# The last 64 output features of a projection as pairs of heads in two 64-column tiles

## The chip, the core and the metric

The kernel runs on one core of a Trainium2 chip. A core has five engines with queues of their own: TensorE (PE in the profile, with its weight loads listed apart as PEld), VectorE (DVE), ScalarE (ACT), GpSimd (POOL) and SyncE (SP), which issues most transfers. Each engine works through its own list of instructions in order and waits on semaphores that the others raise. The metric is the time of one execution on the device in microseconds; lower is better.

## The reference, cut to what matters

A token matrix x of 2048 x 576 goes through four residual layers, A, B, A, B. Layer A is attention over eight dilated neighbours. Layer B, which the change is about, is recurrent: it works on segments of 32 tokens, and eight memory rows come out of one segment and go into the next.

```python
for s in range(n_seg):                                   # 64 segments
    h = jnp.concatenate([mem, xs], axis=1)               # 8 memory rows, 32 tokens
    q, k, v = (jnp.einsum('btd,dhe->bhte', h, W) for W in (Wq, Wk, Wv))   # 32 heads of 128
    p = _softmax(masked(q @ k * scale))
    o = jnp.einsum('bhqk,bhke->bhqe', p, v)
    o = jnp.einsum('bhte,hed->btd', o, Wo)               # the output projection: 32 heads, 576 features
    mem = o[:, :M, :]                                    # the next segment needs these rows
    outs.append(o[:, M:, :])
```

## The kernel before

The two B layers run as two lanes side by side, the second five segments behind the first (`DLY`). There are 64 + 5 = 69 steps (`b_step`). In 59 of them both lanes are at work and a step has 80 columns: 40 of lane 0 and 40 of lane 1 (8 memory rows and 32 tokens each). In the first five and the last five steps only one lane is at work; the operations there are on 40 or 48 columns. The blocks of layer A (`a_tile`) fill in between.

A step consists of these parts, each a function: `qk` (Q and K of all heads, the lines 842 and 845), `vpass` (V, line 889, in four tiles of 32 columns of the array), `scores` (lines 921, 925 and 931, again in tiles of 32 columns), `softmax` on DVE, ACT and POOL, `pv` (line 972, in tiles of 32 rows), and `oproj`, the output projection. `pv` runs twice, for the halves r = 0 and r = 1 of the heads; ACT and DVE copy its results into the tile `OT`.

`oproj` computes psY = sum over 32 heads of Wo[h]^T OT[h]. The 576 output features go onto partitions, so they are five blocks of 128 rows side by side in one PSUM tile `psY`, 80 columns each. 576 is four and a half blocks: the fifth matmul of a head takes 64 features of its own and, as rows 64 to 127, 64 weights of the next head, whose result nobody reads. So a head costs five matmuls of 128x128 weights by 80 columns, and a step 160. They are issued in eight groups (`k` = 0 to 7) of four heads, 20 matmuls each. Group k waits for the copy `o_ev[k]` into `OT`; groups 0 to 3 use the half r = 0 and groups 4 to 7 the half r = 1.

Two functions take the result out of `psY`, both on DVE. `mem_out` (lines 1015 to 1017) copies the memory columns into `hT` of the next step, which its `qk` waits for. `x_out` (line 1035) adds the token columns to the residual stream.

The order of all instructions is fixed when the program is built. `_Plan` is a list scheduler: every operation has an engine, a duration in us that is written in the source, a priority, dependences (`deps`) and buffers. At each moment the free engine takes the ready operation with the lowest priority value; matmuls of another array tiling (`mode`) than the running one pay `SWITCH`. The constants in `PR` shift the priorities of each kind of operation. The plan sets the order only. The waits in the program are put in afterwards by the framework: where an instruction writes or reads a tile that one on another engine has used, it waits for that one, whether the plan named that dependence or not.

Of the kernel before, what the change touches and what calls it, by code (L numbers as in the profile page):

```python
# [8 lines left out]
F32 = mybir.dt.float32  # L9
BF16 = mybir.dt.bfloat16  # L10
ACT = mybir.ActivationFunctionType
ALU = mybir.AluOpType
# [4 lines left out]
P = 128  # L17
SEG = 32
NM = 8
W80 = 80  # L20
# [3 lines left out]
MC = 32  # L24
NH = 32
D = 576
# [25 lines left out]
class _Plan:  # L52
# [41 lines left out]
    def run(self, log=None):  # L94
# [51 lines left out]
        while left:  # L146
            moved = True
            while moved:
                moved = False
                for e, heap in ready.items():  # L150
# [81 lines left out]
def _act(n):  # L232
    return 0.22 + 0.00072 * n
# [13 lines left out]
class _K:  # L247
# [37 lines left out]
    def setup(self):  # L285
        nc, tc = self.nc, self.tc
        cp = self.pool("const", 1)
# [58 lines left out]
        def tiles(name, n, shape, dt=BF16):  # L346
            ts = [wp.tile(shape, dt, name=f"{name}{i}") for i in range(n)]
            self.pl.pool(name, ts)
            return ts
# [13 lines left out]
        tiles("x1", 2, [P, 5, T], F32)  # L363
        tiles("x3", 2, [P, 5, T], F32)
        tiles("x5", 1, [P, 5, T], F32)
        tiles("x0", 1, [P, 640])
        tiles("xs", 1, [P, 5, 2, T])
        tiles("st", 1, [P, 2, T], F32)
# [155 lines left out]
    def a_tile(self, layer, j, dep, due, span):  # L524
# [5 lines left out]
        def pr(f):  # L530
            return due - span * (1.0 - f)
        Q = PR["A"]
        if layer == 1:
# [451 lines left out]
    def oproj(self, t, prios):  # L985

        nc, pl = self.nc, self.pl
        psY = self.psY = pl.buf("r")
        c0, c1 = self.cols(t)
        o = None  # L990
        for k in range(8):
            def mm(e, k=k):
                for h in range(4 * k, 4 * k + 4):
                    for mb in range(5):
                        w0 = h * D + mb * P
                        nc.tensor.matmul(psY.t[:, mb * W80 + c0:mb * W80 + c1], lhsT=self.wo[:, w0:w0 + P], rhs=self.OT[:, h % 16 // 4 * 8 + h // 16 * 4 + h % 4, c0:c1],  # L996
                                         start=(h == 0 and mb == 0), stop=(h == NH - 1 and mb == 4), skip_group_check=True)
            ot = self.ot[k // 4]
            o = pl.op("PE", 0.717 if c1 - c0 == W80 else 0.58, mm, prios[k], [o, self.wo_in[k // 2], self.o_ev[k]],
                      acq=[psY] if k == 0 else (), uses=[ot] if k == 0 else [psY, ot], lat=0.0 if k < 7 else None, mm=20)  # L1000
        return o

    def mem_out(self, t, dep, prio):

        nc, pl, psY = self.nc, self.pl, self.psY
        act = [l for l in range(2) if self.lane_seg(t, l) is not None and self.lane_seg(t + 1, l) is not None]
        if not act or t + 1 >= self.nsteps:
            return
        hT = self.hT[t + 1]
        a, b = act[0] * NM, (act[-1] + 1) * NM  # L1010

        def cp(e):
            y = psY.t[:, 0:5 * W80].rearrange("p (c n) -> p c n", c=5)
            w = slice(MC + a, MC + b)
            nc.vector.tensor_copy(out=hT.t[:, 0:4, w], in_=y[:, 0:4, w])
            nc.vector.tensor_copy(out=hT.t[0:64, 4, w], in_=y[0:64, 4, w])
            nc.vector.tensor_copy(out=hT.t[64:128, 5, w], in_=y[0:64, 4, w])
        o = pl.op("DVE", 0.56, cp, prio, [dep, self.gate[t + 1]], uses=[psY, hT])
        self.mem_in.setdefault(t + 1, []).append(o)

    def x_out(self, t, dep, prio):

        nc, pl, psY = self.nc, self.pl, self.psY
        for lane in range(2):
            s = self.lane_seg(t, lane)
            if s is None:
                continue
            xT, ld, xb = self.acc[lane][s // NS]
            w = slice((s % NS) * SEG, (s % NS + 1) * SEG)

            def add(e, lane=lane, xT=xT, xb=xb, w=w):
                x = xT.t[:, :, w]
                o = x if xb is None else xb.t[:, 0:5 * T].rearrange("p (c n) -> p c n", c=5)[:, :, w]
                c0 = XC[lane]
                nc.vector.tensor_tensor(out=o, in0=x, in1=psY.t[:, 0:5 * W80].rearrange("p (c n) -> p c n", c=5)[:, :, c0:c0 + SEG], op=ALU.add)
            self.x_done[lane][s] = pl.op("DVE", 0.34, add, prio, [dep, ld], uses=[psY, xT] + ([] if xb is None else [xb]))

    def b_step(self, t):
        self.qkt, self.qk_ev, self.PT, self.ot, self.o_ev = {}, {}, {}, {}, []
# [2 lines left out]
        for g in range(11):  # L1042
            self.qk(t, g, t + PR["qk"] + PR["qkd"] * g)
        self.vpass(t, 1, t + PR["v1"])
        self.vpass(t, 0, t + PR["v0"])
# [17 lines left out]
    def trace(self):  # L1063
# [28 lines left out]
        if VERBOSE:  # L1092
# [1 line left out]


DLY = 5
PR = dict(qk=0.371, qkd=0.051, v1=1.416, v0=0.716, w=-0.059, s0=0.01, s1=-1.032, p0=1.091, p1=-1.234, o=0.394,
          od=0.009, mo=0.162, xo=0.923, v2=2.122, a1=2.228, a1s=1.336, a2=0.41, a2s=7.809, fin=5.446, res=-4.695,
          ring=-6.459, A=(0.038, 0.482, 0.789, 0.731, 0.817, -0.034, 0.927, 0.994))
LEAD = 5  # L1100
COPY = 2
HOLD = False
# [58 lines left out]
```

## Time and profile before

| | |
|---|---|
| median of 9 runs | 2158.92 us |
| lowest and highest | 2154.22 and 2161.6 us |
| the profiled execution, its own time | 2162.85 us |
| its span, first to last instruction | 2161.2 us |
| granted TensorE clock, mean over the span | 0.983 |
| `oproj` matmuls (line 996) | 11040, of which 9440 with 80 columns and 1600 with 48 |

The span is the time from the first to the last instruction; 1.65 us of the execution lie around it. The profiled execution is 3.93 us above the median of the runs. A line of a timeline names the start in us, the length, the engine, the line of the source, the operation with its tiles, the shape and how many instructions were merged. Matmuls are pipelined: the length of one is its latency, about 0.2 us, while the next starts much sooner. What a group costs is therefore read from one group's start to the next one's start.

### The profile page before, as it was taken

How to read it: one execution, taken by the hardware profiler on the slowest of the kernel's cores; microseconds unless marked ns; L12 is line 12 of the kernel's file. 1: busy time of each engine (PE TensorE's matmuls, PEld its weight loads, DVE VectorE, ACT ScalarE, POOL GpSimd, SP SyncE). 2: the span in 40 equal slices, each digit the busy share in tenths (PEclk: the TensorE clock that was granted, in tenths of full speed). 3: DMA queues.
4: the chain of work that ended last, by engine and by line, in shares of the span. 5: the costliest groups of instructions: out<-in, count | busy, mean ns of one | idle time of the engine just before them, and what ended most of it. 6: DMA issues, size and time to landing. Idle time of an engine off the chain costs nothing.

```text
span 2161.2 us, 132215 instructions
## 1 busy us (share of the span) xinstructions
PE 2065.2 (96%) x60441; PEld 1733.3 (80%) x60441; DVE 1409.6 (65%) x3545; ACT 1171.8 (54%) x2855; POOL 925.1 (43%) x1310
## 2 busy tenths in 40 slices
PE   3688999999999999999999999999999999999997
PEld 3466888888888888888888888888888888888876
DVE  4556766666667666666766666666666666765674
ACT  2334555555556555555555555555555555554543
POOL 3135454454444444444444454444444444442220
PEclk7889999999999999999999999999999999999999
DMA  9654434343343333333433443344343334332110
GB/s 303 171 172 143 127 114 132 111 130 118 123 125 125 121 122 119 123 125 125 125 109 120 127 133 114 118 125 125 122 122 121 121 120 130 120 124 74 61 58 9
DMA packets 158303, 265.09 MB, mean 123 GB/s; under 512 B 23464, under 2 KB 89904, under 8 KB 157616
## 3 DMA queue, kind: packets, MB, share of 16 engines
q1 hardware_dynamic: 152000, 237.37, 35.4%
q0 software_dynamic: 4576, 18.88, 2.6%
q8 instruction: 472, 7.73, 1.5%
q14 instruction: 87, 0.71, 0.1%
q10 hardware_dynamic: 1168, 0.40, 0.1%
HBM read 240.46 MB, written 16.12 MB: 119 GB/s over the span
## 4 chain that ended last, share of the span: by engine, by line
PE 92%; DMA 4%; DVE 2%; issue 1%; ACT 1%; POOL 0%; SPq 0%; POOLq 0%; ACTq 0%; DVEq 0%
PE r L842 28%; PE r L996 18%; PE r L889 17%; PE r L582 7%; PE r L845 7%; PE r L972 3%; PE r L692 2%; PE r L921 2%; PE r L478 2%; DMA ring<-strip 2%; PE r L925 2%; PE r L656 1%; PE r L931 1%; DMA ring<-in_A_wqkv_dram 1%; PE r L631 1%
## 5 line engine op out<-in xcount | busy, mean ns | idle before, releaser
L842 PE MATMUL r<-hT,wk 128*128 128x80 bf16 (+1 forms) x8832 | 663.4, 199 | 7.8 <-DMA wk<-in_B_Wk_dram 5.9
L842 PE MATMUL r<-hT,wq 128*128 128x80 bf16 (+1 forms) x8832 | 661.3, 198 | 6.6 <-ACT hT L275 3.3
L842 PEld LDWEIGHTS <-wq 128*128 128x128 bf16 x8832 | 502.2, 99 | 39.6 <-issue 26.0
L845 PE MATMUL r<-hT,wqk_r 128*128 128x160 bf16 (+1 forms) x2208 | 507.7, 230 | 0.0
L275 ACT ACTIVATE qk<-r 128x480 bf16<-128x480 f32 (+2 forms) x626 | 332.8, 532 | 320.8 <-PE r L845 311.4
L842 PEld LDWEIGHTS <-wk 128*128 128x128 bf16 x8832 | 447.9, 100 | 7.1 <-DMA wk<-in_B_Wk_dram 6.0
L996 PE MATMUL r<-OT,wo 128*128 128x80 bf16 (+1 forms) x11040 | 422.5, 200 | 10.9 <-issue 6.8
L996 PEld LDWEIGHTS <-wo 128*128 128x128 bf16 x11040 | 396.6, 100 | 29.7 <-issue 16.6
L889 PE MATMUL r<-wv,hT 128*32 128x512 bf16 x5376 | 356.2, 384 | 2.8 <-POOL hT L277 1.7
L282 POOL TENSOR_TENSOR big<-qT,kT 128x512 bf16<-128x512 bf16 (+1 forms) x187 | 312.1, 1689 | 53.9 <-ACT kT L275 43.2
L282 POOL TENSOR_TENSOR ex<-ex,sum 128x384 bf16<-128x384 bf16 x137 | 115.2, 841 | 490.1 <-DVE sum L791 372.1
L282 POOL TENSOR_TENSOR big<-big 128x1280 bf16<-128x1280 bf16 (+1 forms) x66 | 129.9, 1969 | 398.9 <-DVE big L282 344.2
L889 PEld LDWEIGHTS <-hT 128*32 128x32 bf16 x6720 | 167.3, 96 | 136.1 <-issue 4.6
L780 DVE TENSOR_REDUCE nmx<-r 128x4 f32<-128x320 f32 (+1 forms) x276 | 143.1, 518 | 199.6 <-PE r L925 198.1
L275 ACT ACTIVATE V<-r 128x512 bf16<-128x512 f32 x305 | 182.0, 597 | 152.8 <-PE r L889 149.2
L845 PEld LDWEIGHTS <-wqk_r 128*128 128x128 bf16 x2208 | 220.0, 100 | 1.1 <-issue 1.1
L582 PE MATMUL r<-xn,ring 128*128 128x64 bf16 x4725 | 185.5, 194 | 16.7 <-DMA ring<-in_A_wqkv_dram 13.0
L275 ACT ACTIVATE OT<-r 128x320 bf16<-128x320 f32 (+1 forms) x372 | 137.4, 427 | 106.5 <-PE r L972 106.3
L582 PEld LDWEIGHTS <-ring 128*128 128x128 bf16 x4725 | 161.0, 98 | 36.2 <-issue 16.0
L781 DVE TENSOR_TENSOR r<-r,nmx 128x320 f32<-128x320 f32 (+1 forms) x276 | 147.0, 533 | 9.4
L275 ACT ACTIVATE big<-r 128x384 bf16<-128x384 f32 (+1 forms) x322 | 122.7, 450 | 45.4 <-issue 29.9
L277 DVE CAST OT<-r 128x320 bf16<-128x320 f32 (+1 forms) x180 | 76.2, 457 | 92.8 <-PE r L972 92.8
(150 smaller groups left out, 2967.2 us busy)
## 6 DMA issues: line engine op xcount, KB each, us to landing
ring<-strip SPq DMA_DIRECT2D x488, 320.0 KB, 3.4
ring<-strip SPq DMA_DIRECT2D x244, 160.0 KB, 3.8
x1T<-x SPq DMA_DIRECT2D x32, 160.0 KB, 4.1
x<-x1T SPq DMA_DIRECT2D x32, 160.0 KB, 3.4
x3T<-x SPq DMA_DIRECT2D x32, 160.0 KB, 4.0
x<-x3T SPq DMA_DIRECT2D x32, 160.0 KB, 3.6
wo<-in_B_Wo_dram POOLq DMA_DIRECT2D x4, 1152.0 KB, 34.6
wq<-in_B_Wq_dram POOLq DMA_DIRECT2D x2, 2048.0 KB, 17.7
```

The source lines that it names most:

```text
L275: nc.scalar.activation(out=out, in_=in_, func=ACT.Copy, scale=1.0 if scale is None else scale)
L277: (nc.vector if e == "DVE" else nc.gpsimd).tensor_copy(out=out, in_=in_)
L282: (self.nc.vector if e == "DVE" else self.nc.gpsimd).tensor_tensor(out=out, in0=in0, in1=in1, op=op)
L478: nc.tensor.matmul(psf, lhsT=(self.ones if c < 4 else self.ones_h)[:, :], rhs=xs.t[:, c].rearrange("p a t -> p (a t)"), start=(c == 0), st ...
L582: nc.tensor.matmul(ps.t[:, c * T:(c + 1) * T], lhsT=view()[:, kc, w0:w0 + P], rhs=xn.t[:, kc, :], start=(kc == 0), stop=(kc == 4))
L780: nc.vector.tensor_reduce(out=m, in_=v, axis=AX.X, op=ALU.max, negate=True)
L781: nc.vector.tensor_tensor(out=v, in0=v, in1=m.unsqueeze(len(shp) - 1).to_broadcast(shp), op=ALU.add)
L842: nc.tensor.matmul(pv[:, hh, wi, a:b], lhsT=self.Wb[wi][0][:, kc, h * P:(h + 1) * P], rhs=hT.t[:, kc, a:b], start=(hh == 0 and wi == 0 and ...
L845: nc.tensor.matmul(pv[:, hh, :, a:b], lhsT=self.Wb[0][1][:, h * P:(h + 1) * P], rhs=hT.t[:, 4:6, a:b], start=False, stop=(hh == n - 1), sk ...
L889: nc.tensor.matmul(ps.t[c * 32:(c + 1) * 32, :], lhsT=l, rhs=w, start=(kc == 0), stop=(kc == 4))
L972: nc.tensor.matmul(ps[c].t[:, i * n + a - c0:i * n + z - c0], lhsT=V[b].t[q4, r, i, :], rhs=pt.t[q4, i, b, a:z], start=(i == 0 and b == bl ...
L996: nc.tensor.matmul(psY.t[:, mb * W80 + c0:mb * W80 + c1], lhsT=self.wo[:, w0:w0 + P], rhs=self.OT[:, h % 16 // 4 * 8 + h // 16 * 4 + h % 4 ...
```

## The change

The 64 last features get matmuls of their own. A head now has four matmuls of 128x128 weights (features 0 to 511) in its group, 16 a group instead of 20. For features 512 to 575 a new operation `tails` issues, ahead of group 7, 32 matmuls with 128x64 weights, one a head. Even heads put their sum into partitions 0 to 63 of the fifth block of `psY`, odd heads theirs into partitions 64 to 127; these are two tiles of 64 columns of the array, and a new `mode` "D" in the plan. The wanted sum is that of the two.

The odd sum is copied by ACT into a new tile `half` (64 x 80 in SBUF). `mem_out` then copies the four full blocks, adds the two sums twice into `hT` (into chunk 4 and chunk 5), and a last DVE operation adds them in place in `psY`, for `x_out` to read. Three DVE operations a step become four, and there is one more ACT operation. All constants in `PR` have other values.

```diff
+        tiles("half", 1, [P, W80], F32)
...
+        def head(h, out, w0, n, start, stop):
+            nc.tensor.matmul(out, lhsT=self.wo[:, h * D + w0:h * D + w0 + n], rhs=self.OT[:, h % 16 // 4 * 8 + h // 16 * 4 + h % 4, c0:c1],
+                             start=start, stop=stop, skip_group_check=True)
+        tl = slice(4 * W80 + c0, 4 * W80 + c1)
+        half = self.half = pl.buf("half")
         for k in range(8):
+            if k == 7:
+                def tails(e):
+                    for h in range(NH):
+                        head(h, psY.t[h % 2 * 64:h % 2 * 64 + 64, tl], 4 * P, 64, False, h == NH - 1)
+                o = pl.op("PE", 0.6 if c1 - c0 == W80 else 0.48, tails, prios[7], [o, *self.o_ev, self.wo_in[3]],
+                          uses=[psY, *self.ot.values()], mode="D", mm=32)
+                self.half_in = pl.op("ACT", _act(c1 - c0), lambda e: self.copy(e, half.t[0:64, c0:c1], psY.t[64:128, tl]), prios[7] - 0.5, [o],
+                                     acq=[half], uses=[psY])
             def mm(e, k=k):
                 for h in range(4 * k, 4 * k + 4):
-                    for mb in range(5):
-                        w0 = h * D + mb * P
-                        nc.tensor.matmul(psY.t[:, mb * W80 + c0:mb * W80 + c1], lhsT=self.wo[:, w0:w0 + P], ...)
+                    for mb in range(4):
+                        head(h, psY.t[:, mb * W80 + c0:mb * W80 + c1], mb * P, P, h == 0 and mb == 0, h == NH - 1)
             ot = self.ot[k // 4]
-            o = pl.op("PE", 0.717 if c1 - c0 == W80 else 0.58, mm, prios[k], [o, self.wo_in[k // 2], self.o_ev[k]],
+            o = pl.op("PE", 0.573 if c1 - c0 == W80 else 0.464, mm, prios[k], [o, self.wo_in[k // 2], self.o_ev[k]],
...
-            nc.vector.tensor_copy(out=hT.t[:, 0:4, w], in_=y[:, 0:4, w])
-            nc.vector.tensor_copy(out=hT.t[0:64, 4, w], in_=y[0:64, 4, w])
-            nc.vector.tensor_copy(out=hT.t[64:128, 5, w], in_=y[0:64, 4, w])
+            def cp(e):
+                nc.vector.tensor_copy(out=hT.t[:, 0:4, w], in_=psY.t[:, 0:4 * W80].rearrange("p (c n) -> p c n", c=4)[:, :, w])
+            def add(e):
+                for out in (hT.t[0:64, 4, w], hT.t[64:128, 5, w]):
+                    nc.vector.tensor_tensor(out=out, in0=psY.t[0:64, tw], in1=half.t[0:64, w], op=ALU.add)
...
+        self.tail_in = pl.op("DVE", 0.25, lambda e: nc.vector.tensor_tensor(out=psY.t[0:64, tl], in0=psY.t[0:64, tl],
+                                 in1=half.t[0:64, slice(*self.cols(t))], op=ALU.add), prio + 0.01, [dep, self.half_in, o], uses=[psY, half])
...
-PR = dict(qk=0.371, qkd=0.051, v1=1.416, v0=0.716, w=-0.059, s0=0.01, s1=-1.032, p0=1.091, p1=-1.234, o=0.394, ...
+PR = dict(qk=0.6, qkd=0.002, v1=1.831, v0=0.979, w=-0.324, s0=0.23, s1=-1.471, p0=1.099, p1=-1.439, o=0.728, ...
```

More of the change, by code (lines that the diff above doesn't have):

```diff
@@ L990, in oproj @@
         o = None
-        for k in range(8):
+        def head(h, out, w0, n, start, stop):
[3 more added lines that the diff above has]
+        half = self.half = pl.buf("half")
+        for k in range(8):
+            if k == 7:
[6 more added lines that the diff above has]
+                                     acq=[half], uses=[psY])
             def mm(e, k=k):
                 for h in range(4 * k, 4 * k + 4):
-                    for mb in range(5):
-                        w0 = h * D + mb * P
-                        nc.tensor.matmul(psY.t[:, mb * W80 + c0:mb * W80 + c1], lhsT=self.wo[:, w0:w0 + P], rhs=self.OT[:, h % 16 // 4 * 8 + h // 16 * 4 + h % 4, c0:c1],
-                                         start=(h == 0 and mb == 0), stop=(h == NH - 1 and mb == 4), skip_group_check=True)
+                    for mb in range(4):
+                        head(h, psY.t[:, mb * W80 + c0:mb * W80 + c1], mb * P, P, h == 0 and mb == 0, h == NH - 1)
             ot = self.ot[k // 4]
-            o = pl.op("PE", 0.717 if c1 - c0 == W80 else 0.58, mm, prios[k], [o, self.wo_in[k // 2], self.o_ev[k]],
-                      acq=[psY] if k == 0 else (), uses=[ot] if k == 0 else [psY, ot], lat=0.0 if k < 7 else None, mm=20)
+            o = pl.op("PE", 0.573 if c1 - c0 == W80 else 0.464, mm, prios[k], [o, self.wo_in[k // 2], self.o_ev[k]],
+                      acq=[psY] if k == 0 else (), uses=[ot] if k == 0 else [psY, ot], lat=0.0 if k < 7 else None, mm=16)
         return o
@@ L1006, in mem_out @@
         act = [l for l in range(2) if self.lane_seg(t, l) is not None and self.lane_seg(t + 1, l) is not None]
[L1007 to L1019, printed above, removed]
+        half, tl = self.half, slice(*(4 * W80 + c for c in self.cols(t)))
+        o = None
+        if act and t + 1 < self.nsteps:
+            hT = self.hT[t + 1]
+            w = slice(MC + act[0] * NM, MC + (act[-1] + 1) * NM)
+            tw = slice(4 * W80 + w.start, 4 * W80 + w.stop)
+            def cp(e):
[3 more added lines that the diff above has]
+                    nc.vector.tensor_tensor(out=out, in0=psY.t[0:64, tw], in1=half.t[0:64, w], op=ALU.add)
+            a = pl.op("DVE", 0.24, cp, prio, [dep, self.gate[t + 1]], uses=[psY, hT])
+            o = pl.op("DVE", 0.36, add, prio, [dep, self.gate[t + 1], self.half_in], uses=[psY, hT, half])
+            self.mem_in.setdefault(t + 1, []).extend((a, o))
+        self.tail_in = pl.op("DVE", 0.25, lambda e: nc.vector.tensor_tensor(out=psY.t[0:64, tl], in0=psY.t[0:64, tl],
+                                                                           in1=half.t[0:64, slice(*self.cols(t))], op=ALU.add),
+                             prio + 0.01, [dep, self.half_in, o], uses=[psY, half])
     def x_out(self, t, dep, prio):
@@ L1035, in add @@
                 nc.vector.tensor_tensor(out=o, in0=x, in1=psY.t[:, 0:5 * W80].rearrange("p (c n) -> p c n", c=5)[:, :, c0:c0 + SEG], op=ALU.add)
-            self.x_done[lane][s] = pl.op("DVE", 0.34, add, prio, [dep, ld], uses=[psY, xT] + ([] if xb is None else [xb]))
+            self.x_done[lane][s] = pl.op("DVE", 0.34, add, prio, [dep, ld, self.tail_in], uses=[psY, xT] + ([] if xb is None else [xb]))
     def b_step(self, t):
@@ L1096 @@
 DLY = 5
-PR = dict(qk=0.371, qkd=0.051, v1=1.416, v0=0.716, w=-0.059, s0=0.01, s1=-1.032, p0=1.091, p1=-1.234, o=0.394,
-          od=0.009, mo=0.162, xo=0.923, v2=2.122, a1=2.228, a1s=1.336, a2=0.41, a2s=7.809, fin=5.446, res=-4.695,
-          ring=-6.459, A=(0.038, 0.482, 0.789, 0.731, 0.817, -0.034, 0.927, 0.994))
+PR = dict(qk=0.6, qkd=0.002, v1=1.831, v0=0.979, w=-0.324, s0=0.23, s1=-1.471, p0=1.099, p1=-1.439, o=0.728,
+          od=0.004, mo=0.116, xo=0.73, v2=2.249, a1=2.174, a1s=1.577, a2=0.366, a2s=6.308, fin=4.865, res=-3.203,
+          ring=-6.398, A=(-0.2, 0.271, 0.753, 0.551, 0.781, 0.4, 0.994, 0.962))
 LEAD = 5
```

## The prediction

> **What bounds the kernel now.** I read the page first (busy shares, chain), then three stretches of the span, then one step's timeline. The page:
>
> ```profile
> span 2161.2 us, 132215 instructions
> ...
> PE 2065.2 (96%) x60441; PEld 1733.3 (80%) x60441; DVE 1409.6 (65%) x3545; ACT 1171.8 (54%) x2855; POOL 925.1 (43%) x1310
> ...
> PE 92%; DMA 4%; DVE 2%; issue 1%; ACT 1%; POOL 0%; SPq 0%; POOLq 0%; ACTq 0%; DVEq 0%
> ```
>
> PE is busy for 96% of the span and is 92% of the chain that ended last. The stretches (columns: busy us of PE, PEld, DVE, ACT, POOL, then clock, DMA share, GB/s):
>
> ```profile
> 0.00:205.00 205.00, 135.76 (x3963) 106.90 (x3964) 115.80 (x320) 77.02 (x208) 74.25 (x120) 0.86 0.66 203
> 205.00:2100.00 1895.00, 1879.43 (x54788) 1585.46 (x54786) 1260.94 (x3144) 1071.27 (x2584) 845.49 (x1184) 1.00 0.38 118
> 2100.00:2161.00 61.00, 50.03 (x1702) 40.90 (x1698) 32.83 (x84) 23.54 (x65) 5.33 (x7) 0.94 0.03 9
> ```
>
> From 205 to 2100 us PE idles 16 of 1895 us at full clock. There, PE time saved is time saved, and a hole made in PE's list is time lost. Before 205 us PE idles a third of the time. The price list is PE's timeline of one step:
>
> ```profile
> 1009.99 0.33 PE L925 MATMUL r<-qk 128*32 128x80 bf16 x16
> 1010.14 0.43 PE L931 MATMUL r<-qk 128*32 128x48 bf16 x32
> 1010.39 1.06 PE L889 MATMUL r<-wv,hT 128*32 128x512 bf16 x16
> ...
> 1014.97 2.31 PE L996 MATMUL r<-OT,wo 128*128 128x80 bf16 x60
> 1017.22 0.54 PE L972 MATMUL r<-pt,V 32*128 32x48 bf16 x48
> 1017.70 3.76 PE L996 MATMUL r<-OT,wo 128*128 128x80 bf16 x100
> 1021.29 0.89 PE L582 MATMUL r<-xn,ring 128*128 128x64 bf16 x25
> ```
>
> Start to start: 100 full matmuls of 80 columns took 3.59 us, 35.9 ns each. The 60 took 2.25 us, of which 60 x 35.9 ns = 2.15; the other 0.10 us is the change of tiling. L925 is four 32-column tiles at once: 16 matmuls in 0.15 us, a round of four every 37.5 ns, as long as one full matmul. L931, with 48 columns: 32 in 0.25 us, 31 ns a round. In a one-lane step a full matmul costs 0.50 us / 20 = 25 ns (next view).
>
> ```profile
> 2128.83 0.66 PE L996 MATMUL r<-OT,wo 128*128 128x48 bf16 x20
> 2129.33 0.22 PE L740 MATMUL r<-ident,fin 128*128 128x128 bf16 x1
> ```
>
> **The change part by part**
>
> (a) *The tails.* 32 of 160 matmuls of a step become 16 rounds of two tiles. Nothing in the trace has 64-column tiles. The nearest row is L925, with 80 columns and column tiles: 37.5 ns a round, 0.60 us for 16. Bounds: a round can't beat the full matmul's 35.9 ns much (0.57 us); above, if loading grows with the columns of a tile, L931 (32 columns in at most 31 ns) allows 62 ns for 64 columns (0.99 us); if the tiles don't overlap at all, 32 x 35.9 = 1.15 us. I take L925: it loads 4 x 32 = 128 columns a round, as two tiles of 64 do. Full steps: 59 x (1.15 - 0.60) = -32.4 us. One-lane steps, 31 ns a round: 10 x (0.80 - 0.50) = -3.0. Sum -35.4 us.
>
> [...] L925 and L931 show 32-column loads that hide behind their matmuls. [...]
>
> (b) *Changes of tiling.* I counted them in the built order of PE's instructions: 1142 before, 1271 after, since the tails lie mostly between full matmuls (two changes each) and the new constants add about 25. 129 x 0.098 us (0.10 above; drained column tiles show the same) = +12.6 us.
>
> (c) *A new wait.* In the built program the first matmul of group 7 waits for ACT's copy of the odd sum, in 60 of 69 steps: it writes other columns of `psY` than the copy reads, but the same tile. The plan has no such dependence, so nothing keeps PE's list filled: between tails and group 7 there are, in 29 steps, five matmuls of layer A; in 22, eight of the spread (L656); in 7 one-lane steps nothing; elsewhere 20 of V or the like. The nearest chain PE to ACT to PE is this one, columns as before:
>
> ```profile
> 1044.17 0.54 PE L972 MATMUL r<-pt,V 32*128 32x48 bf16 x48
> ...
> 1044.65 0.32 PE L542 MATMUL r<-ident,x 128*128 128x64 bf16 x5
> 1044.77 1.10 ACT L275 ACTIVATE OT<-r 128x320 bf16<-128x320 f32 x3 [0.16 <-PE r L972]
> ...
> 1044.80 0.44 PE L740 MATMUL r<-ident,fin 128*128 128x128 bf16 x5
> ...
> 1045.26 0.73 PE L996 MATMUL r<-OT,wo 128*128 128x80 bf16 x16
> ```
>
> L972 ends at 1044.71, ACT starts 0.06 us later, and its copy of 320 columns takes 0.44 (group view below), so PE goes on 0.05 us after its end. For the half copy the row is 64x64, 0.218 us; I take 0.23 for 80 columns. From the start of the last tail matmul: 0.20 latency + 0.06 + 0.23 + 0.05 = 0.54 us. Cover: 0.036 + 0.098 to leave the tiling, then five A matmuls of 29 ns (25 of them take 0.73 us) = 0.28 us: hole 0.26 x 29 = 7.5 us. With the spread (its eight take 0.23 us at 1027.16, a change included) 0.37: 0.17 x 22 = 3.7. One lane: 0.52 - 0.12 = 0.40 x 7 = 2.8. Sum +14.0 us. ACT's list has nothing unfinished just ahead of the copy in the steps that I followed. Bounds: 0 if the copy is covered, 60 x 0.54 = 32 if nothing covers.
>
> ```profile
> L275 ACT ACTIVATE OT<-r 128x320 bf16<-128x320 f32 x322 | 123.1, 441 | 90.1 <-PE r L972 90.1
> L275 ACT ACTIVATE x<-r 64x64 bf16<-64x64 f32 x27 | 5.9, 218 | 0.0
> L1015 DVE CAST hT<-r 128x64 bf16<-128x64 f32 x58 | 13.0, 224 | 97.5 <-PE r L996 97.3
> L1016 DVE CAST hT<-r 64x16 bf16<-64x16 f32 x58 | 9.0, 155 | 0.0
> L1017 DVE CAST hT<-r 64x16 bf16<-64x16 f32 x58 | 9.7, 167 | 0.8
> ```
>
> (d) *The order behind `pv`.* Group 0 waits for the first copy into `OT`. In the view above that was 1.09 us after the first L972 matmul, with five L542 and five L740 between; these end at 1044.80 + 5 x 0.056 = 1045.08, a hole of 0.18 us, at 25 places. In the new order 24 places have a single L740 matmul there: 0.48 + 0.06 covers 0.54 of 1.09 us, a hole of 0.55 us. 24 x 0.55 - 25 x 0.18 = +8.7 us. Bounds: 0 if the copy comes sooner, 13.2 if the old holes stay in another guise.
>
> (e) *Out of `psY`.* `mem_out` was 0.224 + 0.155 + 0.167 = 0.55 us on DVE; it becomes 0.224 and two small adds of some 0.19 (between 0.155 and L1035's 0.32). With 0.26 us of latency it ends 0.87 us after the last `oproj` matmul starts. The new order has 0.96 us or more of PE work there in nearly all full steps (old: 0.90), and only the ninth matmul of `qk` reads the added part, 0.29 us later: 0. The in-place add delays only `x_out`, with a step to spare; DVE rises by 0.2 us a step from 65%: 0. What it costs if that cover goes is up to 0.3 us a step, 20 us.
>
> (f) *The rest.* SP's list has 992 rows either way, PE's instruction count is equal, POOL loses 26. Before 205 us PE waits for other things, so part of (a) isn't banked: +1.5. "issue" holes at new places: between -2 and +5, I take +1.5.
>
> Sum: -35.4 + 12.6 + 14.0 + 8.7 + 0 + 1.5 + 1.5 = +2.9 us on the profiled 2162.85, 2165.8. The median lies 3.9 us below the profiled execution, so I predict 2158.9 + 2.9 = about 2162 us. What a measurement of this kernel tells from no change is about 0.2%, 4.3 us.
>
> **The rivals**
>
> *R1, faster: the waits are covered.* (c) goes to 0 if the copy ends before group 7's turn, and half of (d) goes: 2.9 - 14 - 4 = -15; with (d) gone wholly, -20. For it: ACT is busy 54% and would be free. Against: two crossings between engines and the copy are 0.34 us even at once. Time 2139 to 2148, centre 2144.
>
> *R2, slower: 64-column loads don't hide.* At 50 ns a round, 16 take 0.80 us: 59 x 0.20 + 10 x 0.30 = +15, total +18, 2177. By the sum, the change loses more than 0.2% from 39 ns a round on (every ns costs 69 x 16 ns = 1.1 us), so this decides early. Against: L925 loads as many columns a round. That the two tiles don't run side by side, so that the change doesn't do what it says, is its far end: 59 x 0.55 + 10 x 0.30 = +35, 2197.
>
> *R3, slower: holes of the new order.* All priorities moved, and the plan doesn't know the waits that the framework adds. If `mem_out`'s cover goes or `pv` waits for the softmax, 0.2 us a step more is +14: 2176. Against: the second scores lead the second `pv` by 6.5 us of PE work (6.8 before, 0.9 of it spare).
>
> **How the numbers follow.** The sum as worked, between -7 and +9 us around 2162 (its own range 2152 to 2168): 0.45. R1 0.25, R2 0.15, R3 0.15. Range: R1's centre inside, R2 at 50 ns inside, far ends out: 2144 to 2182. Faster: R1 and 0.03 of the first, 0.28. Same: 0.24 of the first. Slower: 0.18 of the first, R2 and R3, 0.48.
>
> **What would show it.** Tails: from their first start to the next full matmul 0.7 us (0.60 and a change); over 0.9 is R2. Wait: PE idle in front of group 7, released by ACT `half`, 0.2 to 0.3 us, some 14 us in all; if absent, R1. `pv`: L741's single matmul followed by 0.5 us without a start. `qk`'s ninth matmul waiting for DVE would be R3. Most likely to be wrong: the round time and the size of (c).

## The result, and the profile after

The changed kernel takes 2173.86 us (median of 10 runs, 2171.32 to 2176.07). The kernel before took 2160.16 us (median of 31 runs, 2154.22 to 2166.75). The ratio is 1.0067, with a 95% interval of 1.0058 to 1.0076: slower by 0.7%, 13.7 us. The profiled execution after took 2172.69 us, 9.8 us more than the one before. The medians differ by 13.7; the 3.9 us between these two numbers is how single executions lie about their medians.

The page of the changed kernel, with the same rows as were read before, and below them the matmuls of `oproj` (busy us, mean ns of one, then idle time just before them and what ended it):

```profile
span 2171.0 us, 132394 instructions
...
PE 2052.9 (95%) x60441; PEld 1713.6 (79%) x60441; DVE 1449.3 (67%) x3731; ACT 1155.7 (53%) x2835; POOL 880.5 (41%) x1282
...
PE 88%; DVE 4%; DMA 4%; ACT 2%; issue 1%; POOL 1%; SPq 0%; POOLq 0%; DVEq 0%; ACTq 0%
...
L994 PE MATMUL r<-OT,wo 128*128 128x80 bf16 (+3 forms) x11040 | 407.3, 201 | 28.9 <-ACT OT L275 14.3
```

PE has as many instructions as before and is busy 12.3 us less, in a span that is 9.8 us longer. Its share of the chain that ended last fell from 92% to 88%; DVE, ACT and POOL took over. Idle time in front of `oproj` rose from 10.9 to 28.9 us. The same stretches of the span as before, of the changed kernel (busy us of PE, PEld, DVE, ACT, POOL; then clock, DMA share, GB/s):

```profile
0.00:205.00 205.00, 137.57 (x3958) 110.11 (x3958) 114.95 (x318) 79.38 (x217) 74.34 (x118) 0.84 0.66 201
205.00:2100.00 1895.00, 1858.12 (x54528) 1556.71 (x54524) 1298.67 (x3320) 1049.10 (x2543) 800.82 (x1157) 1.00 0.38 118
```

Between 205 and 2100 us PE now idles 36.9 us; before it was 15.6. The granted clock is the same there (1.00 in both). So the matmuls did get cheaper and the list of PE got holes. Both can be read in one step. First the tails, in PE's timeline of the changed kernel (start, length, engine, line, operation):

```profile
1025.93 1.15 PE L994 MATMUL r<-OT,wo 128*128 128x80 bf16 x40
1027.01 0.32 PE L583 MATMUL r<-xn,ring 128*128 128x64 bf16 x5
1027.40 0.73 PE L994 MATMUL r<-OT,wo 128*128 128x80 bf16 x16
```

The 40 are the last eight matmuls of a group and the 32 tails. From 1025.93 to 1027.01 are 1.08 us; eight full matmuls (0.29) and two changes of tiling (0.19) leave 0.60 us for the tails. The five matmuls of layer A start at 1027.01 and last 0.14 us from start to start; group 7 could start at 1027.16 and starts at 1027.40, a hole of 0.24 us. ACT's timeline in the same place has what it waited for, the copy to `half`:

```profile
1027.12 0.23 ACT L275 ACTIVATE half<-r 64x80 f32<-64x80 f32 x1 [3.23 <-PE r L994]
```

The copy ends at 1027.35 and group 7 goes on 0.05 us later. Second, the place behind `pv` (PE, the same kernel):

```profile
1019.62 0.54 PE L973 MATMUL r<-pt,V 32*128 32x48 bf16 x48
1020.09 0.23 PE L741 MATMUL r<-ident,fin 128*128 128x128 bf16 x1
1020.71 1.88 PE L994 MATMUL r<-OT,wo 128*128 128x80 bf16 x48 [0.38 <-ACT OT L275]
```

One matmul of L741 stands between `pv` and group 0, and group 0 starts 0.62 us after it: 0.06 for the matmul, 0.56 of hole. This happens at 24 places.

The waits of PE between 205 and 2100 us (us in total, times, longest) rose from 14.1 to 32.0 us in all. The groups that matter here, first before and then after (`pt` is what softmax hands to `pv`):

```profile
PE r L996 <- issue: 5.3, 11, 0.9
PE r L996 <- ACT OT L275: 0.6, 2, 0.5
PE r L972 <- DVE pt L799: 0.5, 1, 0.5
```

```profile
PE r L994 <- ACT OT L275: 10.6, 28, 0.5
PE r L994 <- issue: 8.5, 17, 1.0
PE r L973 <- DVE pt L800: 5.2, 7, 1.3
```

The short holes behind the tails don't appear in this view: the modelled latency of the last matmuls (0.2 us) covers most of each, and it has the wait for `half` at one place, with 0.2 us. They have to be read from start to start.

### The profile page after: what moved, and what is told of

Same layout as the page of the kernel before. It is cut to its first block, busy times and chain, and to the rows that moved or that the text cites. A ratio compares the mean times of both kernels' runs of the same rounds, so it can differ in the third digit from the quotient of the medians.

```text
span 2171.0 us, 132394 instructions
## 1 busy us (share of the span) xinstructions
PE 2052.9 (95%) x60441; PEld 1713.6 (79%) x60441; DVE 1449.3 (67%) x3731; ACT 1155.7 (53%) x2835; POOL 880.5 (41%) x1282
## 4 chain that ended last, share of the span: by engine, by line
PE 88%; DVE 4%; DMA 4%; ACT 2%; issue 1%; POOL 1%; SPq 0%; POOLq 0%; DVEq 0%; ACTq 0%
PE r L843 28%; PE r L994 16%; PE r L890 16%; PE r L583 6%; PE r L846 6%; PE r L973 3%; PE r L693 2%; PE r L922 2%; PE r L479 2%; PE r L926 2%; DMA ring<-strip 2%; PE r L932 1%; PE r L657 1%; DMA ring<-in_A_wqkv_dram 1%; PE r L632 1%
## 5 line engine op out<-in xcount | busy, mean ns | idle before, releaser
L275 ACT ACTIVATE qk<-r 128x480 bf16<-128x480 f32 (+2 forms) x619 | 325.8, 526 | 245.2 <-PE r L846 233.0
L994 PE MATMUL r<-OT,wo 128*128 128x80 bf16 (+3 forms) x11040 | 407.3, 201 | 28.9 <-ACT OT L275 14.3
L994 PEld LDWEIGHTS <-wo 128*128 128x128 bf16 (+1 forms) x11040 | 375.2, 103 | 55.1 <-issue 41.7
L282 POOL TENSOR_TENSOR big<-qT,kT 128x512 bf16<-128x512 bf16 x187 | 312.6, 1686 | 49.8 <-ACT kT L275 30.0
L583 PE MATMUL r<-xn,ring 128*128 128x64 bf16 x4725 | 194.0, 194 | 15.4 <-DMA ring<-in_A_wqkv_dram 12.9
L583 PEld LDWEIGHTS <-ring 128*128 128x128 bf16 x4725 | 165.0, 99 | 46.9 <-issue 27.0
L282 POOL TENSOR_TENSOR big<-big 128x1280 bf16<-128x1280 bf16 (+1 forms) x40 | 93.5, 2336 | 201.3 <-DVE big L282 173.9
L277 DVE CAST qk<-r 128x480 bf16<-128x480 f32 (+1 forms) x140 | 89.0, 636 | 98.6 <-PE r L846 69.3
L277 DVE CAST big<-r 128x256 bf16<-128x256 f32 (+1 forms) x220 | 97.1, 477 | 82.7 <-PE r L657 81.6
```

The source lines that it names most:

```text
L275: nc.scalar.activation(out=out, in_=in_, func=ACT.Copy, scale=1.0 if scale is None else scale)
L277: (nc.vector if e == "DVE" else nc.gpsimd).tensor_copy(out=out, in_=in_)
L282: (self.nc.vector if e == "DVE" else self.nc.gpsimd).tensor_tensor(out=out, in0=in0, in1=in1, op=op)
L583: nc.tensor.matmul(ps.t[:, c * T:(c + 1) * T], lhsT=view()[:, kc, w0:w0 + P], rhs=xn.t[:, kc, :], start=(kc == 0), stop=(kc == 4))
L994: nc.tensor.matmul(out, lhsT=self.wo[:, h * D + w0:h * D + w0 + n], rhs=self.OT[:, h % 16 // 4 * 8 + h // 16 * 4 + h % 4, c0:c1], start=st ...
```

## The experiments

Theory T (the prediction's sum): the tails gain what was worked out, and the gain is lost to holes of the new order and to the wait for `half`; whatever covers a hole brings its time back. Its rivals: the holes only move when they are covered, because something else is late next; or the 64-column tiles are themselves the loss. "The changed kernel" is the baseline of a diff where nothing else is said. A group's cost is always read from start to start.

**Old sums in the new order.** The changed kernel's order, made by the plan with all its operations, but `oproj` issues the five full blocks a head as before; tails, copy and adds issue nothing.

```diff
                 def tails(e):
-                    for h in range(NH):
-                        head(...)
+                    pass
...
-                    for mb in range(4):
+                    for mb in range(5):
                         head(h, psY.t[:, mb * W80 + c0:mb * W80 + c1], mb * P, P, ...)
...
-                    nc.vector.tensor_tensor(out=out, in0=psY.t[0:64, tw], in1=half.t[0:64, w], op=ALU.add)
+                    nc.vector.tensor_copy(out=out, in_=psY.t[0:64, tw])
```

> The order of the changed kernel with the arithmetic of the kernel before: no tails, no copy, five matmuls of 128x128 weights a head, and the three copies of mem_out. Theory 1: against the changed kernel +35 us for the full matmuls, -10 for some 104 changes of tiling that go, -10 for the wait that goes: about 2189, which would say that the tails gain some 15 us net and that the new order loses 25 or more against the old one. Rival (the order is as good as the old one, and the tails with what hangs on them are what costs): 2160 or less.

Measured: 2183.82 us, ratio to before 1.0111 (1.0093 to 1.0129), 24 us above before. The order alone costs that much, so the rival (2160 or less) is out. The theory had expected 2189: the new sums gain less than the 15 us that it gave them. With the ratio of the changed kernel (1.0067) the new sums gain 9.5 us net in this order. The 24 holes of 0.56 us behind `pv` are there too (13.4 us; before, 26 of 0.18, 4.7 us), and PE's waits between 205 and 2100 us are 30.2 us.

**New sums in the old order.** Before's plan with its durations, so that the order is before's; the tails are issued at the head of group 7, and the copy to `half` behind group 7, by the same plan operation. The diff is against the kernel before.

```diff
+                if k == 7:
+                    for h in range(NH):
+                        head(h, psY.t[h % 2 * 64:h % 2 * 64 + 64, tl], 4 * P, 64, False, h == NH - 1)
                 for h in range(4 * k, 4 * k + 4):
-                    for mb in range(5):
+                    for mb in range(4):
...
+                if k == 7:
+                    self.copy("ACT", half[0:64, c0:c1], psY.t[64:128, tl])
```

> The order of the kernel before with the new arithmetic: the tails are issued at the head of group 7, the odd sum's copy behind group 7, the adds in place of the copies of mem_out. Theory 1: 59 x 0.55 + 10 x 0.3 us saved, two changes of tiling more in each of 69 steps (13.5 us), no wait on the copy: about -22 us against the kernel before, 2138. Rival (the order that was planned for longer groups leaves later parts short, so that what the tails save turns into waits for softmax or for the memory rows): 2150 to 2160.

Measured: 2150.24 us, ratio 0.9961 (0.9946 to 0.9975): faster than both kernels, by 9 us against before. So the new sums gain 8 to 10 us net in either order, and the order is the rest. That the 64-column tiles are themselves the loss is refuted by this. The time is 12 us above the theory's 2138 and at the lower end of the rival's 2150 to 2160. Of the 22 us of the stream (35.6 for the tails, 138 changes of tiling at 0.098 back) 13 were lost again. PE's waits between 205 and 2100 us rose from 14.1 to 21.5 us, 3.0 of it `pv` waiting for `pt`, as the rival said, and 3.9 of it "issue". Some 6 us stay unassigned. The longest groups:

```profile
PE r L994 <- issue: 7.7, 19, 1.0
PE r L973 <- issue: 5.7, 12, 1.2
PE r L973 <- DVE pt L800: 3.5, 4, 1.6
```

"issue" stands for short holes that wait for nobody; what they are is taken up below.

**The wait for `half` with no cover.** As the last, but the copy is issued ahead of group 7.

```diff
                 if k == 7:
                     for h in range(NH):
                         head(...)
+                    odd()
                 for h in range(4 * k, 4 * k + 4):
                     ...
-                if k == 7:
-                    odd()
```

> The old order of TensorE with the new sums (as the run of the old order before it), but the copy to `half` stands in front of group 7, so that each of the 69 group-7 starts waits for it with nothing of TensorE between. Theory of the prediction: 0.40 us of empty TensorE in each of the 69 steps, 28 us in all beside the run of the old order with the copy behind group 7 (2150), so about 2178, and the groups of waits show group 7 <- ACT half with about 27 us. Rival: the copy's wait also holds up what stands behind it on ACT or takes the place of issue holes; then the difference is under 15 us (below 2165), with the hole seen in fewer places or shorter.

Measured: 2176.5 us, ratio 1.0075 (1.0056 to 1.0094), 25 us above the run before it by the ratios; 2178 was expected. The tile `half` in its trace (who waited for it):

```profile
who waited for it (us, times):
  PE r L994: 22.2, 69
```

And one step of that kernel's timeline, PE and ACT:

```profile
1024.90 0.97 PE L994 MATMUL r<-OT,wo 128*128 128x80 bf16 x35
1025.91 0.23 ACT L275 ACTIVATE half<-r 64x80 f32<-64x80 f32 x1 [2.34 <-PE r L994]
1026.20 0.73 PE L994 MATMUL r<-OT,wo 128*128 128x80 bf16 x16 [0.33 <-ACT half L275]
```

All 69 starts of group 7 wait, where the view shows 22 us and the latency of the last tails hides the rest. By the ends of `oproj` in the two traces the price without cover is 24 us over the 69 steps, 0.35 each; from the tails' start to group 7's it is 0.39 in a full step.

**The copy behind group 7 in the new order.** Only the place of the copy in the program changes; PE's order is the changed kernel's.

```diff
-                self.half_in = pl.op("ACT", _act(c1 - c0), lambda e: self.copy(e, half.t[...], psY.t[64:128, tl]), ...
+                self.half_in = pl.op("ACT", _act(c1 - c0), lambda e: odd("copy"), ...   # whichever comes second issues it
...
+                if k == 7:
+                    odd("group")
```

> The changed kernel with one edit: ACT's copy of the odd sum is issued behind group 7 instead of in front of it, so that group 7 has nothing of ACT's to wait for; the plan and the order of PE stay. Theory 1 (idle PE: the tails gain what they should, and the wait on the copy, the hole behind pv and the changes of tiling eat it): the holes in front of group 7 that the changed kernel's trace shows, 25 of 0.24 us and 22 of 0.17 us, go, about -10 us: 2164. Rival (the holes are only moved: with the copy later, the memory rows of the next step come later and qk waits instead): within 3 us of the changed kernel, 2171 to 2177, with idle time in front of qk.

Measured: 2181.73 us, ratio 1.0096 (1.008 to 1.0112), 6 us slower than the changed kernel by the ratios. The holes in front of group 7 (10.2 us) are gone. A new one has taken their place, in the second part of the spread (PE and ACT, one step of this run):

```profile
935.67 0.23 ACT L275 ACTIVATE half<-r 64x80 f32<-64x80 f32 x1 [4.54 <-PE r L994]
935.71 0.23 PE L657 MATMUL r<-e,epadT 32*128 32x128 bf16 x2
935.92 0.66 ACT L275 ACTIVATE big<-r 128x256 bf16<-128x256 f32 x2
...
936.36 0.34 PE L657 MATMUL r<-e,epadT 32*128 32x128 bf16 x10 [0.42 <-ACT big L275]
```

In ACT's list the copies of `big` stand behind `half`: it ends at 935.90 and they start at 935.92. `half` now waits for the end of group 7, and the spread's matmuls wait for a copy of `big` behind it (0.42 us). That happens at 21 places, 11.9 us in all. So the rival is right in kind, the hole was only moved; it named `qk` for it, and 2171 to 2177 us, and neither came. A wait that is taken from PE and left on ACT came back to PE. The new holes are 1.7 us more than the old ones; the rest of the 6 us is not assigned (the six runs spread from 2175.33 to 2182.61 us, and the profiled one is the longest).

**Five matmuls under the copy of `OT`, three attempts.** At the 24 places behind `pv` five operations of layer A's K projection (25 matmuls of L583, 0.74 us) stand just ahead of `pv`. They are moved behind it, to cover the hole. In the first attempt they stood behind the SP reload of their ring tile.

> The changed kernel with one edit of the order: at the 24 places where pv of the first half is followed by a single transpose matmul and then group 0, the 25 K matmuls of layer A that stand in front of pv are issued behind it. Theory 1: the hole of 0.56 us in front of group 0 is covered by 0.73 us of matmuls, -13 us: 2161. Rival (the time is lost in the start and the end of the program, and a hole closed here opens elsewhere, since layer A's K copy now comes later): less than 5 us gained, 2169 or more.

It took 2216.13 us, but by the order of the program its matmuls read the next strip of weights, so the time can't be compared; that they waited for that strip's transfer is the author's estimate. In the second the reloads and what hangs on the matmuls move with them:

```diff
+                    if i not in late and (e == "SP" or id(o) in after or any(id(b.t) in tiles_ for b in o.acq)):
+                        late.add(i)
...
             o.fn(e)
+            for j in behind.get(i, ()):          # i: the pv operation
+                issued[j][1].fn(issued[j][0])
```

> The changed kernel, but at the 24 places where only one probability multiplication stands between the last projection group's partner and the output copy, the five K matmuls ahead of it are moved behind it, with the ring reloads and the vector work that hang on them. Theory: the 0.56 us hole ahead of the next output group is covered by five K matmuls, 13 us less than the changed kernel, about 2161. Rival: the hole is not gone but changes its place (the ring reload now comes later, and the K matmuls or the qk pair behind them wait), and less than 5 us is gained: 2169 or more.

Measured: 2179.91 us, ratio 1.0096 (1.0079 to 1.0114): slower than the changed kernel. The hole behind `pv` grew from 0.56 to 0.96 us. ACT's timeline of this run says why:

```profile
1025.69 0.44 ACT L298 ACTIVATE kT<-r 128x320 bf16<-128x320 f32 x1 [0.71 <-PE r L606]
1026.02 1.09 ACT L298 ACTIVATE OT<-r 128x320 bf16<-128x320 f32 x3
```

The copy of K now stands ahead of the copies of `OT` in ACT's list, and group 0 waits for K's end as well. The time is in the rival's range, but by another cause than the rival named. The third attempt issues the moved operations in front of group 0 in place of behind `pv`, so ACT has `OT` first:

```diff
-                behind[pe[n]] = pe[n - 5:n]
+                behind[pe[n + 2]] = pe[n - 5:n]
```

> The changed kernel, with the five K matmuls (25 instructions, 0.71 us) at the 24 places set behind `pv` as before in this series, but their copies to SBUF now stand on ACT behind the copies of `OT`, not ahead of them. Theory: with the K matmuls under the `OT` copies the hole of 0.56 us in front of the output group goes, 24 x 0.56 = 13 us; what ends first is the copy of `OT` (0.55 us after pv against 0.71 of K), so nearly all of it is gained and the time is 2160. Rival: the K matmuls, or the vector work that hangs on the K copies, come too late for what follows, and less than 5 us is gained: 2169 or more, with the hole seen ahead of another group.

Measured: 2174.17 us, ratio 1.0051 (1.0035 to 1.0067). The 24 holes are gone, 13.4 us, and by the ratios 3 us are gained, which is not clear of noise, since the two intervals overlap. That is the rival's number. PE's waits between 205 and 2100 us in this run, to be read beside those of the changed kernel above:

```profile
PE r L1020 <- issue: 14.6, 25, 1.5
PE r L998 <- DVE pt L825: 7.0, 8, 1.8
PE r L606 <- issue: 4.3, 4, 2.2
PE r L606 <- DMA ring<-strip: 3.7, 7, 1.0
PE r L998 <- issue: 2.6, 5, 0.7
...
PE r L1020 <- ACT OT L298: 0.9, 3, 0.3
```

(L1020, L998 and L606 are L994, L973 and L583 of the changed kernel.) The wait for `OT` is gone. What took its place is "issue": no semaphore, no engine. Over all lines "issue" went from 10.9 to 22.2 us. The waits for the ring went from 1.6 to 4.7 and those for `pt` from 5.2 to 7.0. So most of what came back are the "issue" holes. This division is that of the profiled execution, the longest of the six (2177.99 us, 5.3 above the changed kernel's), and not of the median.

**What "issue" is.** One such hole in that run:

```profile
809.45 1.17 PE L1020 MATMUL r<-OT,wo 128*128 128x80 bf16 x28
811.59 1.59 PE L1020 MATMUL r<-OT,wo 128*128 128x80 bf16 x52 [0.98 <-issue]
```

It stands inside a row of matmuls with the same operands. In order of the program most of these holes are 128 matmuls or a multiple apart (896 again and again, which is about one step). The DMA rows of each kernel here have this queue, with 472 packets or, in the two kernels below with more matmuls, 473 (packets, MB, share of the DMA time):

```profile
q8 instruction: 472, 7.73, 1.5%
```

472 packets of 16,384 bytes, for PE's 120,882 loads and matmuls (2 x 60441). If the queue carries these alone, that is 256 instructions a packet, 64 bytes each: 128 matmuls with their loads, an estimate from the two counts. By the times of these packets in the trace, 34 of the 39 holes of over 0.15 us between matmuls of one line (205 to 2100 us) end 2.3 to 2.9 us after the start of such a packet and 1.2 to 1.7 us after its end, and the 128 matmuls ahead of them had run in 3.4 us (median), against 4.6 on average. The author's reading of these times: PE had used up a block of its list, and what stood in the next packet could run only 1.2 to 1.7 us after that packet's end.

The kernel's own source reckons with this. In `_Plan` PE may not enter the next 256 instructions of its list (`PAGE`) before a time for their transfer has passed (`FETCH`, a constant of the plan). So the orders were planned with the ends of blocks in view, but not for matmuls that are moved afterwards, as in this series, nor for new sums in an old order.

This was put to the test with 75 harmless matmuls in the idle time at 6 us (the five 8 x 8 transposes of the first memory, sixteen times), which shift all later instructions against the blocks.

```diff
-            for c in range(5):
+            for c in [n % 5 for n in range(80)]:
                 nc.tensor.matmul(ps.t[:, c * NM:(c + 1) * NM], lhsT=row[:, c * P:(c + 1) * P], ...)
```

> The previous kernel with the K matmuls under the copies (five K matmuls behind `pv`, their copies last), and 75 repeated matmuls of 8 x 8 in the idle time at 6 us, so that every later instruction of TensorE stands 75 matmuls further on in its list. Theory (the unnamed holes are the list itself arriving late: it comes in 472 blocks of 16 KB, 128 matmuls with their loads each, and a block that runs in about 3.3 us is over before the next is there): all 36 holes of more than 0.15 us leave their places and stand 75 matmuls earlier in the program's order (53 later), at the new block ends; as blocks shorter than 3.4 us fall from 32 to 25, the holes sum to 15 to 21 us in place of 23 and the time to 2166 to 2173. Rival: the holes belong to their places in a step (an operand or a buffer that the trace does not name); then they stay at the same matmuls, and the time is that of the kernel without the 75, 2172 to 2176.

Measured: 2170.49 us, ratio 1.0052 (1.0033 to 1.0071). The place of the holes of over 0.15 us that end behind a packet as above, counted in matmuls and modulo 128:

```
                          holes   sum us   place in PE's list   place in the order without the 75
changed kernel              21      9.8         77 to 89                77 to 89
K under the copy            34     20.5         77 to 92                77 to 92
the same, 75 more           29     15.5         77 to 91                 2 to 16
```

The holes kept their place in the list and left their matmuls. (In each kernel the place falls steadily over the execution, from about 90 to 77, which is why it is a range.) That they belong to the list's blocks and not to an operand is shown by this. The kernel before has such holes too: 26 of its 28 between matmuls of one line end behind a packet in the same way, 11.9 us. "issue" fell from 22.2 to 16.1 us; the time is in the theory's range, 2166 to 2173, but the ratio is that of the run without the 75 (1.0051). Part of the 6 us can lie in which execution was profiled, so what a good alignment is worth stays open.

**The old order, shifted.** The kernel of the old order with the new sums, and the same 75 matmuls.

> The old order with the new sums (2150) and the same 75 repeated matmuls at 6 us. Theory: the list's block ends move; blocks under 3.7 us fall from 69 to 54, the 7 us of such holes become 3 to 7 us, so 2146 to 2151. Rival: no effect of the shift beyond the 3 us that the repeated matmuls may cost at the start: 2150 to 2154.

Measured: 2149.88 us, ratio 0.9964 (0.9952 to 0.9977), no change to its 0.9961. "issue" fell from 15.4 to 12.3 us, too little to be seen in the time.

**Two new orders.** In the first the copy to `half` stands behind group 7 in the plan too, and the constants of the plan are chosen anew. In the second the tails are also part of group 7.

```diff
 # first: after the loop over k
-                self.half_in = pl.op("ACT", ..., [o], acq=[half], uses=[psY])      # behind the tails
+        self.half_in = pl.op("ACT", ..., [o], acq=[half], uses=[psY])              # behind group 7
-PR = dict(qk=0.6, qkd=0.002, v1=1.831, ...
+PR = dict(qk=0.448, qkd=0.097, v1=2.392, ...
 # second, as well
-                o = pl.op("PE", 0.6 if c1 - c0 == W80 else 0.48, tails, prios[7], ...)
+                if k == 7:                                                          # inside mm of group 7
+                    for h in range(NH):
+                        head(...)
-PR = dict(qk=0.6, qkd=0.002, v1=1.831, ...
+PR = dict(qk=0.155, qkd=0.105, v1=1.765, ...
```

> The new sums, with the copy to `half` behind group 7 in the plan itself, and the planner's constants chosen again for that plan, so that the order is a third one. By its list it has 1339 changes of tiling (before 1144), 195 more, +19 us, against -35 us for the tails: 16 us less than before if the holes come out as before, about 2143. Theory (the sums gain, an order with the holes covered keeps the gain): faster than before, between 2140 and 2152. Rival: any new order pays the holes and the start again, as the changed kernel's order does (+24 with the old sums); then it is at 2160 or more.

> The tails at the head of group 7 as one operation in the plan, the copy to `half` behind it, both known to the planner, and its constants chosen again. Changes of tiling by the list: 1293, against 1282 in the old order with the new sums. Theory: the stream is 36 us less for the tails and 15 more for changes of tiling than before, 21 less; of that, some 10 us are lost to holes of the instruction list as in the other runs, so 2145 to 2153. Rival: a third order pays its start and its list as the replanned one did, 2165 or more.

Measured: the first 2173.4 us, ratio 1.0055 (1.0041 to 1.007), as slow as the changed kernel, where 2140 to 2152 was expected; the second 2150.39 us, ratio 0.9965 (0.9952 to 0.9977), as fast as the old order with the new sums and in its expected range. The first has 23.2 us of "issue" between 205 and 2100 us, twice the 11.5 of before, and only 9.7 us of other waits; it also has the most changes of tiling, 1339 against 1144. The second has 14.4 us of "issue" and 1293 changes. That this is what separates the two is not shown: no run changed one of them alone. The best time in this study is thus 2150 us, 0.4% below before, in three kernels that keep the tails at the head of group 7 and the copy to `half` behind it. Theory T is right that the gain is lost in the new order and wrong about the way back: in that order, neither of the two holes that were closed brought its time back.

## Why the prediction was right, and where it was not

The time, 2173.86, lies in the range (2144 to 2182), and "slower" had the largest chance. Part of that is luck. The sum itself gave +2.9 us, too little to be told from no change, and 13.7 were measured. Its own range, -7 to +9 us on the time before (2152 to 2168; "around 2162" doesn't fit these ends), doesn't hold that. The time lies in the range because of the room made for R2, which the runs refute, and for R3, whose 2176 came near although the wait in every step that it priced did not come. The mechanisms of (a) to (e) were right; one term, the rest, was far too small.

- **(a), the tails, right.** From the first tail to the next instruction are 0.70 us, so 16 rounds took 0.60 without the change of tiling; from the first start to the 32nd are 0.563 us, a round every 36 ns (L925 had given 37.5). In one-lane steps a round took 32 ns. That makes 35.6 us, -35.4 predicted.
- **R2, refuted.** The loads of the changed kernel, by shape (busy us, mean ns):

```profile
L994 PEld LDWEIGHTS <-wo 128*128 128x128 bf16 x8832 | 330.0, 100 | 48.5 <-issue 39.8
L994 PEld LDWEIGHTS <-wo 128*64 128x64 bf16 x2208 | 45.2, 114 | 6.6 <-issue 1.9
```

  A 64-column load is 114 ns long, and two tiles still start every 36 ns. No run shows the 50 ns a round at which R2 was priced.
- **(b), changes of tiling, right.** The count is 1273 against 1144 in the lists, and a change still adds 0.096 to 0.098 us from start to start: 12.6 us. The list of the old sums in the new order has 1169, so 25 come from the order, as predicted.
- **(c), the wait for `half`, right in kind, a little high.** Holes of 0.24 us at 28 places, nearly all with five A matmuls (6.4 us; 0.26 x 29 predicted), and of 0.17 us at 22 with the spread (3.8; 3.7 predicted). The 2.8 us of one-lane steps didn't come: there the copy is issued behind group 7. 10.2 us in place of 14.0. R1 had these waits covered; they are not. The run without cover measured 0.35 to 0.39 us a step, against the 0.40 taken for a start without cover.
- **(d), behind `pv`, right.** 24 holes of 0.56 us against 0.55 predicted, 13.4 us; 26 of 0.18 before, 4.7. The difference is the 8.7 us of the prediction.
- **(e), out of `psY`, right.** PE's waits for `hT` of `mem_out` are 0.6 us between 205 and 2100 us.
- **(f), the rest, wrong: the step that failed.** It had +3.0 us. What was measured for (a) to (d) sums to -35.6 + 12.6 + 10.2 + 8.7 = -4.1 us (-0.1 predicted), and the profiled executions differ by +9.8, so the rest is 14 us (18 by the medians, which differ by 13.7). The rise in PE's waits between 205 and 2100 us, without "issue" and without the wait for `OT` that is (d), is 8.5 us (from 2.0 to 10.5), 4.7 of it `pv` waiting for `pt`. These are single waits, of the kind that R3 named, but not the `pv` and `qk` of every step that it priced. The wait for `pt` is not the order's alone: it is 2.4 us with the old sums in the new order and 3.5 with the new sums in the old one (0.5 before). 5.4 us stay unassigned. By the ends of `oproj` in the two traces, the changed kernel is 1.1 us ahead at step 4, 5.7 behind at step 7, 4.3 behind at step 8, 7.0 at step 58 and 9.6 at the last: nearly half of the loss comes up in three steps near the start, and 2.6 us in the last ten. The old sums in the new order have the early loss too (4.1 us at step 8), the new sums in the old order don't. So the order makes it; which of its moves does was not tested. Between 205 and 320 us, where these steps lie, PE waits 4.5 us in the changed kernel and 1.2 before; the longest of these is 1.1 us for DVE's copy into `OT`. The last ten steps are different: the new sums in the old order lose 2.9 us there, the old sums in the new order 1.1. "issue", also in (f), cost nothing here: 10.9 us after, 11.5 before.

The runs put the division differently from the sum: the order costs 24 us (the prediction's parts of it: (d), 25 of the changes, 3 of (f), 14 us), and the new sums gain 8 to 10 us in either order, tails, changes of tiling, waits and list together.

## What to carry to other kernels

Separate the order from the arithmetic: run the old sums in the new order and the new sums in the old one, since a scheduler with retuned constants can cost more than the edit gains (24 us against 8 to 10 here). Put the wait that the framework adds (same tile, other columns) where the waiting engine has other work, and look at what stands behind it in the in-order list of the engine that copies. When a covered hole gives nothing back, look at whether the waits have turned into "issue" at multiples of a block of instructions (128 matmuls here): with K under the copy such holes took 20.5 us at 34 places, where the changed kernel had 9.8 at 21.

## What the runs showed of the hardware

- PE's list arrives in packets of 16,384 bytes (472 in the kernel before and in the changed one, 1.1 us each on average). A packet starts, at the median, when PE has run about a fifth of the block ahead of it, with the blocks' ends taken from the places of the holes (24 of 128 matmuls before, 29 in the changed kernel). Blocks that PE runs through in about 3.4 us, where the average is 4.6, are followed, in some places, by holes: 26 of 0.16 to 1.27 us before, 21 of 0.15 to 1.02 us in the changed kernel. With K under the copy, a covered wait, there are 34, and the list has 472 packets as before.
- Two tiles of 64 columns run side by side at 36 ns a round with 80 columns, the pace of one full matmul (35.9 ns), although each load lasts 114 ns (changed kernel).
- From PE through a small copy on ACT and back to PE is 0.53 us from start to start in the changed kernel where nothing else is waited for: 0.24 until the copy starts, 0.24 of copy of 80 columns, 0.05 after its end. 0.54 had been predicted. With 48 columns it is 0.49 by an estimate from 0.23, 0.21 (the copies of 48 columns) and 0.05.
